# Diagonal convolution ahead, x1 and the first modal convolution between the taps: an interleaved state-space kernel on Trainium2

## The chip, the cores and the metric

The program runs on one core of one Trainium2 chip, in one launch, in fp32. The metric is device microseconds of that core. The engines are PE (TensorE matmul; PEld is its weight load), DVE (VectorE), ACT (ScalarE), POOL (GpSimd) and SP (SyncE, which issues nearly all transfers).

## The reference

```python
def _A_ref(q, k, v, shift_k, ssm_k, ssm_D):          # 2048 x 512
    ...                                              # k_shift: causal depthwise convolution of k, 4 taps
    kv = k_shift * v
    y = irfft(rfft(kv, 2 * S) * rfft(ssm_k, 2 * S))  # long causal convolution, channel by channel
    return q * (y + kv * ssm_D)

def _B_ref(u, log_A_real, A_imag, C_real, C_imag, log_dt, D_skip):
    A = -exp(log_A_real) + 1j * A_imag               # 512 channels x 128 modes
    C = (C_real + 1j * C_imag) * dt
    K = 2 * einsum("dn,dnl->dl", C, exp(A * dt * pos)).real      # the taps: 512 x 2048
    return irfft(rfft(u) * rfft(K)) + u * D_skip

x = A_q
x = x + _A_ref(_layernorm(x), ...)    # x1
x = x + _B_ref(_layernorm(x), ...)
x = x + _A_ref(_layernorm(x), ...)    # x2
x = x + _B_ref(_layernorm(x), ...)
```

The diagonal convolution y of kv is the same in both uses of A, and K is the same in both uses of B. So there is one diagonal convolution, one generation of K, two modal convolutions and two gated updates, x1 and x2.

## The kernel before

A convolution is a four-step FFT on PE with DVE's 32x32 transposes between steps, one quarter of the channels (128) at a time. The forward step (`fwd_group`, L173) multiplies by constant matrices and transposes into a spectrum tile z. Then come eight chunks: `f2_chunk` (L193) finishes the transform into PSUM (pu); ACT writes the swapped half into sw (L276, L277); DVE multiplies pu by the kernel's spectrum kab into vv (L278); POOL multiplies sw (L280), and POOL or DVE adds (L281); PE transforms back (pi, L290), ACT copies (L291). The way back out is four transposes into w (L305) and four pairs of matmuls (po, L311), each followed by the caller's `finish`. `convolution` (L250) writes this out as steps, with the chunks of neighbouring quarters overlapping.

Work before the convolutions:

- `taps` (L542) makes K in 64 taps of 8 channels by 4 and half the modes: exponentials (`mags`, L461, in batches of eight taps on ACT), rounded angles (`angles`, L474), sines (`waves`, L486), products on POOL and DVE (`products`, L497: L504, L505, L506, L508) and matmuls (`contract`, L511), whose result goes to DRAM.
- `spectrum_quarter` (L220) turns a quarter of a kernel into its spectrum, and DRAM holds it; for the modal kernel it can start when that quarter's 16 taps are in DRAM.
- `diagonal` (L658) is, in order: 48 steps of the four diagonal spectra, with the gates (`gated`, L600, which makes kv) and row statistics among them, and 59 steps of the diagonal convolution, whose output goes to DRAM (ya_d).

`run_steps` (L852) walks through two generators in turn, one step of `stream` (taps, and after each tap one step of a modal spectrum, if one is waiting) and two of `diagonal`. When both have ended come x1 (`gated_update`, L697: 16 row tiles, each gated with the loaded ya, then squares and statistics; `normalizer`, L203, twice), the first modal convolution (L831) and then, in new pools, x2 and the second modal convolution.

The written order is not the order of the engines. A planner simulates the program and orders each engine's instructions by priority (the written order) and by the time when operands and buffers are ready in its own clock; a tile is given out once all users of the buffer's earlier tile have ended. On the chip each engine and SP then go through their queues in that fixed order. `after` adds an order without a wait, which keeps exponentials and sines in batches on ACT.

Memory decides what can overlap: the pool `conv_a` of the diagonal part lies on the right side, and x takes its place; the pools of the taps lie on the left until `gctx.close()`. Of the eight PSUM banks, three are for convolutions ("c1"), two each for magnitudes and modal spectra ("pm") and for angles ("pa"), one for the taps' result.

Of the kernel before, what the change touches and what calls it, by code (L numbers as in the profile page):

```python
# [9 lines left out]
F32 = mybir.dt.float32  # L10
# [3 lines left out]
AF = mybir.ActivationFunctionType  # L14
# [85 lines left out]
def kernel(ctx: ExitStack, tc: tile.TileContext, out, x_in, kv_in, ssmk_in, ssmd_in,  # L100
# [5 lines left out]
    def sbuf(stack, name, side="left"):  # L106
        return stack.enter_context(tc.tile_pool(name=name, bufs=1, side=side, reuse_waits="tile"))
# [320 lines left out]
    psum["pm"] = (pp, NPM)  # L428

# [15 lines left out]
    NM1 = 9  # L445
    NM2 = 5
# [88 lines left out]
    zlast_k, todo = [], []  # L535
# [41 lines left out]

    def stream():
        for _ in taps():
            if todo and next(todo[0], 0) == 0:  # L580
                todo.pop(0)
            yield
        while todo:
            if next(todo[0], 0) == 0:
                todo.pop(0)
            yield


    with ExitStack() as actx:
# [100 lines left out]
    xp = sbuf(ctx, "xp", "right")  # L690
    x = xp.tile([128, 16, 512], F32, name="x")
    st = xp.tile([128, 16, 4, 6], F32, name="st")
    w1.append(xp.tile([128, 128], F32, name="w1"))
    nc.sync.dma_start(w1[0], w1_in)
    st_all = lambda t: st[:, t, :, :].rearrange("p q s -> p (q s)")

    def gated_update(buffer, spare, rnd, load_x=False):  # L697
        yas = []
# [41 lines left out]
    own = [(xp, "ut", 3)] * 3  # L740
# [5 lines left out]
    with ExitStack() as yctx:  # L746
        yp = sbuf(yctx, "yp", "right")
        normalized(gated_update(lambda k: yp.tile([128, 16, 4, 32], F32, name="yaq", tag="yaq", bufs=NYA),
                                own + [(yp, "ut", 16 - 4 * NYA)] * (16 - 4 * NYA), 0, True))
# [52 lines left out]
    def finish_b(rnd, q, g, po):  # L802
        xs = x[:, :, 128 * q + 32 * g:128 * q + 32 * g + 32]
        yo = xs
        if rnd == 1:
            pool, tag, bufs = own[0]
            yo = pool.tile([128, 16, 32], F32, name="yo", tag=tag, bufs=bufs)
# [23 lines left out]
    first = conv_b(0)  # L831
    for _ in range(2 * NCH):
        next(first)
    gctx.close()
    pctx.close()
# [10 lines left out]
    normalized(gated_update(lambda k: rotating("u", [128, 16, 4, 32], "yaq", 3),  # L846
                            own + [(pools["conv"], "vv", NSB)] * NSB + [(pools["conv"], "sw", NSB)] * NSB, 1))
    for _ in conv_b(1):
        pass


def run_steps(gens):  # L852
    gens = list(gens)
    while gens:
        for item in list(gens):
            for _ in range(item[1]):
                try:
                    next(item[0])
                except StopIteration:
                    gens.remove(item)  # L860
                    break
# [53 lines left out]
```

## Time and profile before

| what | us |
|---|---|
| median of 3 runs | 804.04 |
| lowest, highest | 797.04, 807.67 |
| the profiled execution | 805.59 |
| its span, first to last instruction | 803.8 |
| busy in the span: PE, DVE, POOL, ACT | 635.2, 621.3, 533.7, 477.7 |

Numbers of the profile come from that one execution. A row of grouped instructions gives line, engine, operation, output<-inputs, shapes, count, then busy time, mean length of one in ns, and the engine's idle time ahead of them with what ended it. Rows of one line give minimum, median and maximum in ns and the first and last start. Rows of stretches give from:to, length, then busy time and count for each engine, then the clock that was granted to PE, the DMA engines' share and GB/s; if only one line's instructions are asked for, one busy time stands there.

### The profile page before, as it was taken

What the parts mean: (1) busy time and instruction counts of PE and PEld (TensorE: products, weight loads), DVE (VectorE), ACT (ScalarE), POOL (GpSimd) and SP (SyncE); (2) the same over time, 40 slices, a digit from 0 to 9 for tenths busy, and PEclk for the clock granted to TensorE, in tenths of its full rate; (3) what the DMA queues carried; (4) which work ended last, traced back from release to release, by engine and by line L of the source; (5) the groups of instructions that cost most, each with busy time, mean ns of one, the idle gap of its engine ahead of it and who ended that gap; (6) DMA issues with size and microseconds to landing.
All of it is one profiled execution on the core that took longest, in us unless ns stands there. A gap on an engine that the chain in (4) does not pass through costs nothing. (4 is left out here: it accounts for less than half of the span.)

```text
span 803.8 us, 14448 instructions
## 1 busy us (share of the span) xinstructions
PE 635.2 (79%) x5064; PEld 447.3 (56%) x5064; DVE 621.3 (77%) x939; ACT 477.7 (59%) x879; POOL 533.7 (66%) x496
## 2 busy tenths in 40 slices
PE   3378696688799989999889863599789750998996
PEld 2255565356567747767556442386657620476673
DVE  7757979998967967647759499845668889878776
ACT  4035355345378875776785765649746525878573
POOL 4965778776778965838956277316665836288783
PEclk9676599868999999999899665789989995899999
DMA  9577177367477463664441593147987642068792
GB/s 326 188 247 270 40 241 254 108 200 254 146 215 203 127 182 110 182 171 123 115 131 34 174 341 105 46 129 199 233 200 183 159 103 54 1 164 223 201 252 105
DMA packets 89612, 135.47 MB, mean 169 GB/s; under 512 B 8508, under 2 KB 37700, under 8 KB 89028
## 3 DMA queue, kind: packets, MB, share of 16 engines
q1 hardware_dynamic: 88644, 132.13, 56.5%
q0 software_dynamic: 896, 2.43, 1.1%
q8 instruction: 40, 0.66, 0.4%
q14 instruction: 32, 0.26, 0.1%
HBM read 98.87 MB, written 35.65 MB: 167 GB/s over the span
## 5 line engine op out<-in xcount | busy, mean ns | idle before, releaser
L280 POOL TENSOR_TENSOR sw<-sw,kab 128x512 f32<-128x512 f32 x96 | 124.4, 1302 | 67.6 <-ACT sw L277 59.6
L196 PEld LDWEIGHTS pu<-zu,w 128*128 128x128 f32 x768 | 95.7, 193 | 52.9 <-DVE vv L278 18.6
L196 PE MATMUL pu<-zu,w 128*128 128x128 f32 x768 | 109.5, 285 | 15.1 <-DVE vv L278 12.8
L504 POOL TENSOR_TENSOR xy<-tt,m 128x512 f32<-128x512 f32 x64 | 84.9, 1327 | 53.5 <-ACT tt L493 23.8
L171 PE MATMUL pf<-kk,wz 128*128 128x256 f32 x256 | 86.3, 481 | 41.8 <-POOL kk L236 25.3
L278 DVE TENSOR_TENSOR vv<-pu,kab 128x512 f32<-128x512 f32 x96 | 64.9, 679 | 63.9 <-ACT sw L277 27.0
L290 PE MATMUL pi<-vv,mm 128*128 128x128 f32 x768 | 107.3, 285 | 3.5 <-DVE vv L278 2.6
L281 POOL TENSOR_TENSOR vv<-vv,sw 128x512 f32<-128x512 f32 x76 | 98.8, 1303 | 13.6 <-DVE vv L278 10.3
L290 PEld LDWEIGHTS pi<-vv,mm 128*128 128x128 f32 x768 | 96.5, 197 | 15.0 <-issue 9.1
L276 ACT ACTIVATE sw<-pu 64x512 f32<-64x512 f32 x96 | 57.0, 594 | 63.3 <-PE pu L196 60.8
L171 PEld LDWEIGHTS pf<-kk,wz 128*128 128x128 f32 x256 | 56.7, 237 | 62.3 <-POOL kk L236 33.3
L491 ACT ACTIVATE tt<-pa 128x512 f32<-128x512 f32 x64 | 38.3, 599 | 82.1 <-PE pa L483 72.3
L196 PE MATMUL pu<-zk,w 128*128 128x128 f32 x512 | 78.3, 307 | 6.4 <-DVE zk L191 4.2
L196 PEld LDWEIGHTS pu<-zk,w 128*128 128x128 f32 x512 | 72.7, 217 | 15.6 <-DVE zk L191 6.3
L505 DVE TENSOR_TENSOR tt<-tt,m 128x512 f32<-128x512 f32 x64 | 79.9, 1248 | 0.9 <-ACT tt L493 0.4
L244 ACT COPY pc<-pu 128x512 f32<-128x512 f32 x64 | 37.4, 591 | 57.3 <-PE pu L196 35.3
L506 DVE SCALAR_TENSOR_TENSOR xy<-tt,m 128x256 f32<-128x256 f32 x64 | 51.5, 805 | 25.7 <-ACT tt L492 15.3
L468 ACT ACTIVATE m<-pm 128x512 f32<-128x512 f32 x96 | 53.8, 604 | 22.6 <-PE pm L466 21.6
L483 PE MATMUL pa<-y,minus 128*128 128x512 f32 x64 | 37.1, 588 | 32.0 <-DVE y L482 30.5
L311 PE MATMUL po<-w,w 128*64 128x512 f32 x192 | 55.4, 655 | 7.3 <-DVE w L305 7.0
L519 PE MATMUL pk<-xy,tt 128*32 128x64 f32 x2048 | 50.5, 242 | 13.3 <-DVE ks L529 9.0
L519 PEld LDWEIGHTS pk<-xy,tt 128*32 128x32 f32 x2048 | 37.7, 122 | 39.1 <-issue 28.9
(139 smaller groups left out, 1295.4 us busy)
## 6 DMA issues: line engine op xcount, KB each, us to landing
kab<-spec SPq DMA_DIRECT2D x188, 256.0 KB, 4.0
spec<-pc SPq DMA_DIRECT2D x64, 256.0 KB, 2.7
kvt<-kv_in SPq DMA_DIRECT2D x16, 624.0 KB
yaq<-ya_d SPq DMA_DIRECT2D x8, 1024.0 KB, 10.6
kk<-ssmk_in SPq DMA_DIRECT2D x16, 256.0 KB, 2.9
kv_d<-u SPq DMA_DIRECT2D x16, 256.0 KB, 7.5
kdram<-ks SPq DMA_DIRECT2D x64, 64.0 KB, 1.8
kk<-kdram SPq DMA_DIRECT2D x16, 256.0 KB, 2.7
```

The lines of the kernel that those rows point to most:

```text
L171: yield T.matmul(o, w, rhs, start=True, stop=True)
L196: ins = T.matmul(pu[:, i, :], w2[:, c * CK + i, :], z[:, :, c * CK + i, :], start=True, stop=True)
L276: S.mul(sw[0:64], pu[64:128], -1.0)
L278: V.tensor_mul(vv, pu, kabs[s][:, 0])
L280: (V if last else G).tensor_mul(sw, sw, kabs[s][:, 1])
L281: (V if last or s % add_dve == add_dve - 1 else G).tensor_add(vv, vv, sw)
L290: i1s[t] = T.matmul(pi[:, i, :], mm[:, c * CK + i, :], vvs[t][:, i, :], start=True, stop=True)
L311: ins = T.matmul(po[64 * a:64 * a + 64], w4, ws[g][:, :, 16 * a:16 * a + 16, :].rearrange("p x t r -> p t x r"), start=True, stop=True, ti ...
L468: i = S.activation(m, pm, AF.Exp)
L504: G.tensor_mul(xy[:, :, :, 32:64], tt[:, :, :, 1:33], m1[:, :, 32:64][:, None].to_broadcast([128, 2, 8, 32]))
L505: (G if (4 * gi + k) % E2P == E2P - 1 else V).tensor_mul(e2, e2, m2[:, None].to_broadcast([128, 2, 8, 32]))
L519: T.matmul(pk[32 * i4:32 * i4 + 32, 2 * k + i, :], e2[:, r, 4 * i + i4, :], xy[:, r, 4 * i + i4, :], start=r == 0, stop=r == 1, tile_posit ...
```

## The change

`run_steps` goes. One generator, `main`, now holds the diagonal part, x1 and a newly written first modal convolution, `conv_b0`, and it takes three steps for each step of `stream` while the stream's step number is under 34, then two. x's pool is opened when the diagonal pool is closed, while the taps' pools stay open.

`conv_b0` works quarter by quarter with one z: the results of the way back replace z's chunks in place, and the next quarter's z is a new tile in the same buffer. Chunks have a lag of one, kab three buffers (the w tiles of the way out take theirs too), sw and vv two. A quarter begins its chunks when its modal spectrum has been written (`spectra`). It uses the full-height forward matrices throughout, where the earlier one used half-height ones from its second quarter on. Quarters 0 to 2 use the "c1" banks; the last one uses the taps' banks for pi and po. Row statistics of quarter q - 1 and the normalization of q + 1 go with the chunks of q. To make room, the magnitudes get 8 and 4 buffers in place of 9 and 5, and raw rows one in place of two.

```diff
-    NM1 = 9
-    NM2 = 5
+    NM1 = 8
+    NM2 = 4
...
-        raw = wk.tile([128, 2, 128], F32, name="raw", tag="raw", bufs=2)
+        raw = wk.tile([128, 2, 128], F32, name="raw", tag="raw", bufs=1)
...
-        RT = 1
-        RD = 2
-        diag = diagonal()
-        for _ in range(4):
-            next(diag)
-        run_steps([(stream(), RT), (diag, RD)])
...
+        yield from diagonal()
+        actx.close()
...
+    def conv_b0():
...
+        NK0 = 3
+        LAG0 = 1
...
+        def load(q, c):
+            kab = bp.tile([128, 2, CK, 128], F32, name="kab", tag="kab", bufs=NK0)
+            for h in range(2):
+                nc.sync.dma_start(kab[64 * h:64 * h + 64].rearrange("p r k c -> p r (k c)"),
+                                  spec[1][q][c].rearrange("(r k) x -> k r x", r=2))
...
+        def chunk(q, c):
+            kab = kabs[q, c]
+            pu, _ = f2_chunk(zs[q], c)
+            sw = bp.tile([128, CK, 128], F32, name="sw", tag="sw", bufs=2)
+            vv = bp.tile([128, CK, 128], F32, name="vv", tag="vv", bufs=2)
+            S.mul(sw[0:64], pu[64:128], -1.0)
+            S.copy(sw[64:128], pu[0:64])
+            V.tensor_mul(vv, pu, kab[:, 0])
+            G.tensor_mul(sw, sw, kab[:, 1])
+            (V if c % 3 == 2 else G).tensor_add(vv, vv, sw)
+            vvs[q, c] = vv
+
+        def back(q, c):
+            pi = bank("pi", "pa" if q == NQ - 1 else "c1").rearrange("p (k c) -> p k c", k=CK)
+            for i in range(CK):
+                T.matmul(pi[:, i, :], mm[:, c * CK + i, :], vvs[q, c][:, i, :], start=True, stop=True)
+            S.copy(zs[q][:, :, c * CK:(c + 1) * CK, :], pi.rearrange("p k (x r) -> p x k r", r=2))
...
+        for q in range(NQ):
+            zs[q] = bp.tile([128, 64, 32, 2], F32, name="zu", tag="z", bufs=1)
+            for g in range(4):
+                fwd_group(lambda ps_, j, n: us[q][ps_, :, 32 * g + j:32 * g + j + n], zs[q], 32 * g, 32, 16)
+                yield
+            while spectra[0] <= q:
+                yield
+            for c in range(-2, NCH + LAG0):
+                if c + 2 < NCH:
+                    load(q, c + 2)
+                if 0 <= c < NCH:
+                    chunk(q, c)
+                    if q < NQ - 1:
+                        norm(q + 1, c)
...
+                if c >= LAG0:
+                    back(q, c - LAG0)
+                if c >= 0:
+                    yield
+            for g in range(5):
+                if g < 4:
+                    turn(q, g)
+                if g > 0:
+                    out_group(q, g - 1)
+                yield
...
+    steps = main()
+    for _ in range(4):
+        next(steps)
+    RD = lambda n: 3 if n < 34 else 2
+    n = 0
+    for _ in stream():
+        for _ in range(RD(n)):
+            next(steps, None)
+        n += 1
+    for _ in steps:
+        pass
+    gctx.close()
+    pctx.close()
...
-    first = conv_b(0)
-    for _ in range(2 * NCH):
-        next(first)
-    gctx.close()
-    pctx.close()
...
-    for _ in first:
-        pass
```

`turn` and `out_group` are the transposes into w and the output matmuls, whose sum DVE adds to x.

More of the change, by code (lines that the diff above doesn't have):

```diff
@@ L428 @@
     psum["pm"] = (pp, NPM)
+    psum["pa"] = (pp, NPA)
     for tag, bufs in (("c1", 7 - NPA - NPM), ("pa", NPA), ("pk", 1)):
@@ L533, in contract @@
                 ks[32 * i4:32 * i4 + 32].rearrange("p (s t) c -> p s (t c)", s=4))
-    zlast_k, todo = [], []
+    zlast_k, todo, spectra = [], [], [0]
     EORD = 3
@@ L576, in taps, with spectrum_step, first_half @@
             yield
+    def spectrum_step():
+        if todo and next(todo[0], 0) == 0:
+            todo.pop(0)
+            spectra[0] += 1
     def stream():
         for _ in taps():
-            if todo and next(todo[0], 0) == 0:
-                todo.pop(0)
+            spectrum_step()
             yield
         while todo:
-            if next(todo[0], 0) == 0:
-                todo.pop(0)
+            spectrum_step()
             yield
-    with ExitStack() as actx:
+    def first_half():
+        actx = ExitStack()
         ap = sbuf(actx, "conv_a", "right")
@@ L739 @@
     HN = 8
-    own = [(xp, "ut", 3)] * 3
+    own = lambda: [(bq, "ut", 3)] * 3
     def normalized(rows):
@@ new lines, in main @@
+    def main():
+        yield from first_half()
+        open_x()
+        with ExitStack() as yctx:
+            yp = sbuf(yctx, "yp", "right")
+            yield from normalized(gated_update(lambda k: yp.tile([128, 16, 4, 32], F32, name="yaq", tag="yaq", bufs=NYA),
+                                               [(yp, "ut", 7)] * 7, 0, True))
+        yield from conv_b0()
+    steps = main()
[7 more added lines that the diff above has]
+        n += 1
@@ L805, in finish_b @@
         if rnd == 1:
-            pool, tag, bufs = own[0]
+            pool, tag, bufs = own()[0]
             yo = pool.tile([128, 16, 32], F32, name="yo", tag=tag, bufs=bufs)
@@ L845 @@
         normalizer(t0, HN, st_all)
-    normalized(gated_update(lambda k: rotating("u", [128, 16, 4, 32], "yaq", 3),
-                            own + [(pools["conv"], "vv", NSB)] * NSB + [(pools["conv"], "sw", NSB)] * NSB, 1))
+    for _ in normalized(gated_update(lambda k: rotating("u", [128, 16, 4, 32], "yaq", 3),
+                                     own() + [(pools["conv"], "vv", NSB)] * NSB + [(pools["conv"], "sw", NSB)] * NSB, 1)):
+        pass
     for _ in conv_b(1):
         pass
[L852 to L861, printed above, removed]
 def _seq(a):
```

59 lines of the change are left out of this document (48 added, 11 removed).

## The prediction

> **What bounds the kernel now.** I read the page's busy shares first, then cut the span where the work changes (gates and spectra, diagonal convolution, x1, first modal convolution, and after x2 the second) and asked for busy time by stage.
>
> ```profile
> span 803.8 us, 14448 instructions
> PE 635.2 (79%) x5064; PEld 447.3 (56%) x5064; DVE 621.3 (77%) x939; ACT 477.7 (59%) x879; POOL 533.7 (66%) x496
> ```
> ```profile
> 40.00:230.00 190.00, 151.01 (x1276) 106.37 (x1277) 168.48 (x222) 87.94 (x152) 135.32 (x129) 0.82 0.61 198
> 230.00:465.00 235.00, 216.27 (x2059) 152.61 (x2057) 161.07 (x220) 172.91 (x300) 159.34 (x149) 0.94 0.51 146
> 465.00:517.00 52.00, 26.22 (x305) 17.75 (x305) 51.45 (x74) 28.11 (x61) 38.34 (x30) 0.63 0.54 162
> 517.00:657.00 140.00, 117.93 (x733) 87.44 (x732) 94.30 (x174) 84.72 (x165) 78.61 (x74) 0.94 0.65 166
> 693.00:804.00 111.00, 99.14 (x647) 69.04 (x646) 80.42 (x111) 73.67 (x140) 75.52 (x69) 0.99 0.63 171
> ```
>
> The columns are window, length, then busy time of PE, PEld, DVE, ACT and POOL, and the granted clock. S1 (gates, first kernel's spectra, taps) has DVE at 168 of 190. S2 (diagonal convolution and taps) has PE at 216 of 235, 92%. S3 (x1 and the last taps) has DVE at 51.5 of 52 and PE at half. S4 (last modal spectrum, first modal convolution) has PE at 118 of 140, 84%. Last, the second modal convolution has PE at 99 of 111, 89%. What DVE's time is made of, its rows tell:
>
> ```profile
> L505 DVE TENSOR_TENSOR tt<-tt,m x64: 643/1163/4292, 72.4 to 508.5; 128x512 f32<-128x512 f32 x64
> L506 DVE SCALAR_TENSOR_TENSOR xy<-tt,m x64: 375/462/3491, 71.4 to 512.8; 128x256 f32<-128x256 f32 x64
> L504 POOL TENSOR_TENSOR xy<-tt,m x64: 1171/1200/1718, 72.1 to 506.4; 128x512 f32<-128x512 f32 x64
> L508 POOL TENSOR_TENSOR xy<-tt,m x64: 667/880/1222, 73.2 to 508.0; 128x256 f32<-128x256 f32 x64
> L608 DVE TENSOR_TENSOR u<-kvt x15: 643/1145/2369, 18.2 to 218.3; 128x512 f32<-128x512 f32 x15
> L721 DVE SCALAR_TENSOR_TENSOR x<-ut,rs,x x32: 694/741/1950, 475.9 to 689.0; 128x512 f32<-128x512 f32 x32
> ```
>
> The same DVE instruction takes 643 ns or 4292 (minimum, median, maximum): DVE operations that read two SBUF tiles stretch, POOL's hardly do. I read that as DVE waiting for POOL, so I add POOL's busy time to DVE's two-input operations at their minimum. S1 has 25 taps (rows below) and some 14 gates of four such operations: 135 + 25 x 1.02 + 14 x 4 x 0.643 = 197 us in 190. S3: 38 + 6 x 1.02 + 16 x 0.694 = 56 in 52. Both are full. S4: 78.6 + 10 additions on DVE at L608's 0.643 = 85 in 140, so 61%. [...]
>
> How the taps and modal spectra lie in the stages (DVE's rounding, one for each tap; ACT's spectrum copies, eight a quarter, 32 of the first 36 being the other kernel's):
>
> ```profile
> 40.00:230.00 190.00, 16.55 (x25) 0.82 0.61 198
> 230.00:465.00 235.00, 21.80 (x33) 0.94 0.51 146
> 465.00:517.00 52.00, 3.91 (x6) 0.63 0.54 162
> ```
> ```profile
> 40.00:230.00 190.00, 21.29 (x36) 0.82 0.61 198
> 230.00:465.00 235.00, 9.33 (x16) 0.94 0.51 146
> 465.00:517.00 52.00, 2.12 (x4) 0.63 0.54 162
> 517.00:657.00 140.00, 4.68 (x8) 0.94 0.65 166
> ```
>
> **The change, in terms of PE and of that pair.** No computation goes away. In written order the diagonal part now gets three steps a tap, not two: its 48 steps of spectra and gates are through at tap 15, its 59 of convolution at tap 34. Then x1 takes taps 34 to 42, and the first modal convolution's quarters start at about 44, 53, 62 and, after the last spectrum, behind the taps. So S1 gives up taps, S2 too, and S4 gets them. PE's prices come from S2, grouped by line:
>
> ```profile
> L290 PE MATMUL pi<-vv,mm 128*128 128x128 f32 x256 | 37.3, 290 | 0.3 <-POOL vv L281 0.2
> L196 PE MATMUL pu<-zu,w 128*128 128x128 f32 x255 | 36.1, 282 | 0.6 <-DVE zu L191 0.5
> L171 PE MATMUL pf<-u,wz 128*128 128x256 f32 x96 | 26.8, 405 | 0.3 <-DVE zu L191 0.3
> L466 PE MATMUL pm<-tg,rw 64*128 64x512 f32 x58 | 26.8, 528 | 3.1 <-ACT m L468 2.5 <-ACT pc L244 0.6
> L519 PE MATMUL pk<-xy,tt 128*32 128x64 f32 x1056 | 24.6, 228 | 3.6 <-POOL xy L508 2.8 <-DVE y L482 0.8
> L196 PE MATMUL pu<-zk,w 128*128 128x128 f32 x144 | 21.1, 294 | 0.2 <-ACT m L468 0.2
> L311 PE MATMUL po<-w,w 128*64 128x512 f32 x64 | 19.8, 700 | 2.3 <-DVE w L305 2.3
> L483 PE MATMUL pa<-y,minus 128*128 128x512 f32 x33 | 17.7, 537 | 4.5 <-DVE y L482 4.3 <-ACT tt L491 0.2
> L171 PE MATMUL pf<-kk,wz 128*128 128x256 f32 x64 | 17.1, 395 | 1.5 <-DVE zk L191 1.4
> L478 PE MATMUL pa<-tt,rw 64*128 64x512 f32 x33 | 15.4, 490 | 2.4 <-ACT tt L492 2.4
> ```
>
> A tap: (26.8 + 24.6 + 17.7 + 15.4) / 33 = 2.56. A spectrum quarter: 64 x 21.1/144 + 17.1/2 = 17.9. A convolution quarter: (37.3 + 36.1 + 19.8)/4 + 26.8/3 = 32.2. All rows add to 243, PE was busy 216, since modelled spans of neighbours overlap: times 0.89, so 2.28, 16.0 and 28.7.
>
> - S1 loses 10 taps. It is full on the pair, and a tap takes 1.171 + 0.667 + 0.643 + 0.375 = 2.86 of it: 29 us, so 161.
> - S2 goes from 33 taps to 19 and from 2 spectrum quarters to 1.2: 14 x 2.28 + 0.8 x 16.0 = 45 us of PE, at 92% 49 us, so 186.
> - S3: x1 still waits for the whole diagonal output (layer norm over all channels) and for its loads. It stays at 52 with 6 taps beside it, because the pair is full with those. x1 ends at 40 + 161 + 186 + 52 = 439, not 517: 78 us earlier.
> - S4 gets 64 - 15 - 19 - 6 = 24 taps (54.7 us of PE), 1.3 more spectrum quarters (20.8), and a dearer forward step: quarters 1 to 3 used the half-array form below, 13.9/3 = 4.6 a quarter, and now take the 128x256 form, 8.9 x 0.89 = 8.0: 10 us. So 117.9 + 86 = 203 us of PE in place of 118. Its mix is now S2's, taps beside a convolution, so I take S2's 92%: 221 us, ending at 660. At the last stage's 89% it ends at 667, at S4's own 84% at 681.
>
> ```profile
> L171 PE MATMUL pf<-u,w 64*128 64x512 f32 x48 | 13.9, 629 | 0.0
> ```
>
> What follows 657 (statistics, x2, second convolution, 147 us) stays. The sum is +3 us on the profiled execution's 805.6 (1.8 outside the span): 809. Of the runs shown, 804.04 is the median, 1.6 below that execution.
>
> Costs that I put at nothing, with what covers them:
>
> ```profile
> kab<-spec SPq DMA_DIRECT2D x188, 256.0 KB, 4.0
> yaq<-ya_d SPq DMA_DIRECT2D x8, 1024.0 KB, 10.6
> ```
> ```profile
> ACT pc L244 <- DMA spec<-pc: 20.5, 7, 7.2
> ```
> ```profile
> L210 ACT ACT_TABLE_LOAD x2 | 2.6, 1283 | 0.0
> ```
>
> Eight magnitude buffers instead of nine, four instead of five: the last exponential of each batch of eight taps now waits for the previous tap's products, with ACT's sines and the convolution's copies queued behind it. Fewer buffers can gain nothing; the upper end is 8 batches x (1.20 + 0.88) = 17 us; I take 0, since some ten exponentials go ahead of it and ACT is 74% busy in S2. One raw buffer: 0, a load has four taps' time. x1's two square roots now fall among sines: 0 to two table loads each, 4 x 1.283 = 5.1, hidden by the pair in S3. The 64 kab loads of the first modal convolution move on SP in among row loads, tap stores and spectrum stores; a load waits there for one of three kab buffers, which the transposes use too, and behind it stand the stores that ACT's copies wait for. Those waits are 20.5 us now; from minus a few (two stores fewer at S4's start) to another 20.5; I take 0, as the diagonal convolution runs beside the taps with three such buffers. In front of x2 the new pool lies on the finished convolution's memory: 0 to one late load, 10.6; 0, for x2's second load is first used by its fifth row. Two additions move from DVE to POOL and two output groups the other way: under 3 us on engines with room.
>
> **The rivals.** *Faster: x1 gets filled.* If S3 took 14 taps, not 6 (PE's idle 25.8 us there would hold the 8 x 2.28 = 18), S4 loses 18/0.92 = 20 us: 789. If S4 then also reaches 95%, 203 - 18 = 185 takes 195 and not 201: 783. For it: before's S3 took every tap that was left, and 30 are now in stock. Against it: the pair, at 56 of 52. [...] Chance 0.27.
>
> *Slower: one z buffer makes the quarters a chain.* Each quarter's forward step now waits for the last transpose of the quarter before it, and two sw/vv buffers allow two chunks in flight.
>
> ```profile
> L276 ACT ACTIVATE sw<-pu 64x512 f32<-64x512 f32 x96 | 57.0, 594 | 63.3 <-PE pu L196 60.8 <-POOL vv L281 0.6 <-POOL sw L280 0.4
> L280 POOL TENSOR_TENSOR sw<-sw,kab x32: 1258/1282/1469, 232.2 to 423.1; 128x512 f32<-128x512 f32 x32
> L281 POOL TENSOR_TENSOR vv<-vv,sw 128x512 f32<-128x512 f32 x76 | 98.8, 1303 | 13.6 <-DVE vv L278 10.3
> L305 DVE STREAM_TRANSPOSE w<-ie 128x1024 f32<-128x1024 f32 x32 | 38.2, 1222 | 3.1 <-ACT ie L291 3.1
> L813 DVE TENSOR_TENSOR x<-x,po 128x512 f32<-128x512 f32 x14 | 9.5, 677 | 3.8 <-PE po L311 3.7
> ```
>
> A chunk is 8 matmuls each way (2 x 1.1), two ACT halves and a copy (3 x 0.59), two POOL operations (1.28 + 1.30): 6.6 us, so one each 3.0 with two in flight. A quarter alone: 8 x 3.0 + 3.6 + 8.0 forward + 4 x 1.22 + 1.9 to leave = 42. Beside taps S2's chunks came each 190.9/31 = 6.2 us, which makes 67. Two quarters beside taps and two behind them: 218, ending at 657, beside PE's 660. Once a third quarter runs at the tap pace, 25 us more: 685, +28, so 834; S4's own 84% gives 681, 830. It decides when the second quarter's last output comes later than the last tap. For it: both ends touch already, and S2 had two z buffers where this has one. Against it: PE would idle, and the taps would then be through sooner. Chance 0.29.
>
> *It doesn't do what it says.* The planner orders each engine by its own clock, and taps ran ahead of the written order before (58 begun by 465, against 52). If they do so wholly, the quarters come behind all taps: 4 x 42 = 168 in place of 140, plus 10 for the forward form: 843. Only the taps' own buffers hold them, but three wave tiles bind early. Chance 0.03.
>
> **How the numbers follow.** 809 is the likeliest, at 0.41, with its own range 797 to 820 (densities of 95% to 89% give 802 to 816, the small terms 4 or 5 more either way). Below it stands the filled x1, 783 to 789; above it the chain, 830 to 834, and the last, 843. About 0.1 is left out at each end by 780 to 838. What this measurement can tell from no change is 2%, so 788 to 820. Faster 0.27, within 0.41, slower 0.29 + 0.03 = 0.32.
>
> **What would show it.** In the changed profile, x1 should end near 439; taps after x1's end 24 in number; PE in the stretch from x1's end to the first convolution's end busy some 203 us at 92%; DVE's two-input products again between 0.64 and several us. POOL and two-input DVE time well under the stage's length in x1 while more than ten taps run there would make the first rival true. Chunks of the third quarter at 6 us and PE under 85% would show the chain. A last chunk of the first quarter behind the last tap would show the third. I am wrong at the root if S1 and S2 don't shorten by about 29 and 49 us, since all that S4 pays for comes from there.

## The result, and the profile after

The changed kernel takes 880.55 us (median of four runs, 871.81 to 886.3) against 802.79 for the kernel before beside it (797.04 to 807.67): a ratio of 1.0935, with a 95% interval of 1.0808 to 1.1062. One of the four executions of the changed kernel, 886.3, was in a slower state, and the ratio and its interval leave it out. The forecast was 809 us, 838 at the upper end. Below, times within the kernel and the bounds of stages belong to the profiled execution of after, 883.1 us with a span of 881.2.

The page's busy shares of after:

```profile
span 881.2 us, 14583 instructions
PE 667.0 (76%) x5112; PEld 477.5 (54%) x5112; DVE 624.9 (71%) x939; ACT 479.5 (54%) x879; POOL 535.1 (61%) x492
```

PE has 32 us more to do, DVE and POOL have nearly what they had; the span is 77 us longer. The stretches of after, cut where the same work begins and ends (window, length, then PE, PEld, DVE, ACT, POOL, clock, DMA share, GB/s):

```profile
40.00:230.00 190.00, 147.12 (x1275) 103.96 (x1274) 169.71 (x220) 85.45 (x149) 137.25 (x128) 0.81 0.61 199
230.00:465.00 235.00, 218.15 (x2040) 154.06 (x2039) 165.15 (x219) 168.62 (x291) 162.49 (x148) 0.93 0.50 140
465.00:519.00 54.00, 34.34 (x292) 22.12 (x293) 48.91 (x76) 36.33 (x71) 41.54 (x33) 0.56 0.65 192
519.00:735.00 216.00, 144.50 (x815) 114.33 (x813) 97.13 (x187) 84.69 (x164) 72.58 (x66) 0.84 0.36 93
768.00:881.00 113.00, 100.08 (x647) 69.72 (x645) 81.05 (x113) 73.71 (x140) 75.48 (x69) 0.98 0.61 168
```

S1 and S2 are what they were, within 4 us of PE's busy time. x1 ends at 519, where it ended at 518. The first modal convolution, S4, takes 216 us in place of 140 and PE is busy in 67% of it: 76 of the 77 us lie here. The taps of after, by stage (DVE's rounding, one a tap):

```profile
40.00:230.00 190.00, 16.49 (x25) 0.81 0.61 199
230.00:465.00 235.00, 21.69 (x33) 0.93 0.50 140
465.00:519.00 54.00, 3.90 (x6) 0.56 0.65 192
```

25, 33 and 6, exactly as before, and none beside the convolution. The text of the program now puts 15 taps beside the gates and spectra and 24 behind x1; the engines' order does not. So nothing was interleaved, and the newly written convolution had to run alone. What its engines wait for there (total us, times, longest):

```profile
DVE vv L792 <- ACT sw L791: 76.0, 28, 7.8
POOL sw L793 <- ACT sw L791: 68.6, 18, 18.1
PEld pi L800 <- POOL vv L794: 42.6, 17, 8.7
...
ACT zu L801 <- PE pi L800: 32.4, 22, 3.7
ACT u L770 <- PE pf L171: 31.1, 3, 15.5
```

Every engine waits for the one before it in a chunk's chain: ACT's swapped halves, POOL's product and addition, PE's way back, ACT's copy. The first quarter's end in the timeline (start, length, engine, line) shows the change to the second:

```profile
576.94 1.77 PE L800 MATMUL pi<-vv,mm 128*128 128x128 f32 x8 [2.42 <-POOL vv L794]
578.75 0.59 ACT L801 COPY zu<-pi 128x512 f32<-128x512 f32 x1 [3.60 <-PE pi L800]
579.37 3.50 DVE L805 STREAM_TRANSPOSE w<-zu 128x1024 f32<-128x1024 f32 x3 [4.44 <-ACT zu L801]
...
580.76 5.32 PE L811 MATMUL po<-w,w 128*64 128x512 f32 x16 [2.05 <-DVE w L805]
...
586.01 3.72 PE L171 MATMUL pf<-u,wz 128*128 128x256 f32 x16
...
590.92 3.84 PE L171 MATMUL pf<-u,wz 128*128 128x256 f32 x16 [1.19 <-DVE zu L191]
...
594.80 6.26 ACT L770 ACTIVATE u<-x,nb,rs 128x128 f32<-128x128 f32 x16 [15.46 <-PE pf L171]
...
601.07 0.59 ACT L790 ACTIVATE sw<-pu 64x512 f32<-64x512 f32 x1
```

After the last chunk come way back, copy, four transposes, output, the next forward step, and then all 16 normalizations of the quarter after that, on ACT, before its first swapped half: 28 us from the last swapped product of one quarter (574) to the first of the next (602). Before took 1 to 4 (the last and first products of neighbouring quarters on POOL).

### The profile page after: what moved, and what is told of

Same layout as the page of the kernel before. It is cut to its first block, busy times and chain, and to the rows that moved or that the text cites. A ratio compares the mean times of both kernels' runs of the same rounds, so it can differ in the third digit from the quotient of the medians.

```text
span 881.2 us, 14583 instructions
## 1 busy us (share of the span) xinstructions
PE 667.0 (76%) x5112; PEld 477.5 (54%) x5112; DVE 624.9 (71%) x939; ACT 479.5 (54%) x879; POOL 535.1 (61%) x492
## 5 line engine op out<-in xcount | busy, mean ns | idle before, releaser
L505 POOL TENSOR_TENSOR xy<-tt,m 128x512 f32<-128x512 f32 x64 | 87.6, 1369 | 49.3 <-ACT tt L494 35.9
L196 PEld LDWEIGHTS pu<-zu,w 128*128 128x128 f32 x768 | 99.6, 200 | 32.3 <-issue 9.6
L171 PE MATMUL pf<-kk,wz 128*128 128x256 f32 x256 | 83.6, 471 | 40.2 <-POOL kk L236 26.7
L506 DVE TENSOR_TENSOR tt<-tt,m 128x512 f32<-128x512 f32 x64 | 82.2, 1285 | 0.9 <-ACT tt L494 0.8
L171 PE MATMUL pf<-u,wz 128*128 128x256 f32 x264 | 71.1, 412 | 11.7 <-DVE zu L191 5.4
L800 PE MATMUL pi<-vv,mm 128*128 128x128 f32 x256 | 43.6, 326 | 46.3 <-POOL vv L794 39.3
L281 POOL TENSOR_TENSOR vv<-vv,sw 128x512 f32<-128x512 f32 x54 | 70.6, 1310 | 10.5 <-DVE vv L278 8.7
L290 PE MATMUL pi<-vv,mm 128*128 128x128 f32 x512 | 72.9, 288 | 0.7 <-POOL vv L281 0.3
L290 PEld LDWEIGHTS pi<-vv,mm 128*128 128x128 f32 x512 | 65.2, 199 | 9.0 <-issue 4.5
L507 DVE SCALAR_TENSOR_TENSOR xy<-tt,m 128x256 f32<-128x256 f32 x64 | 56.9, 890 | 16.6 <-ACT tt L493 15.0
L800 PEld LDWEIGHTS pi<-vv,mm 128*128 128x128 f32 x256 | 38.3, 230 | 50.7 <-POOL vv L794 42.6
```

The costliest lines, as they stand in the source:

```text
L171: yield T.matmul(o, w, rhs, start=True, stop=True)
L196: ins = T.matmul(pu[:, i, :], w2[:, c * CK + i, :], z[:, :, c * CK + i, :], start=True, stop=True)
L281: (V if last or s % add_dve == add_dve - 1 else G).tensor_add(vv, vv, sw)
L290: i1s[t] = T.matmul(pi[:, i, :], mm[:, c * CK + i, :], vvs[t][:, i, :], start=True, stop=True)
L505: G.tensor_mul(xy[:, :, :, 32:64], tt[:, :, :, 1:33], m1[:, :, 32:64][:, None].to_broadcast([128, 2, 8, 32]))
L506: (G if (4 * gi + k) % E2P == E2P - 1 else V).tensor_mul(e2, e2, m2[:, None].to_broadcast([128, 2, 8, 32]))
```

## Experiments

The place of the quarters tells most. Below, from the traces: the end of x1, the start on POOL of each quarter's first swapped product, and the end of the last addition to x.

| kernel | end of x1 | first products of the four quarters | end | median us |
|---|---|---|---|---|
| before | 518 | 545, 571, 598, 626 | 657 | 802.8 |
| after | 519 | 549, 602, 654, 701 | 733 | 880.6 |
| e1_rd2 | 519 | 550, 603, 655, 702 | 734 | 879.2 |
| e8_rd9 | 492 | 526, 589, 641, 687 | 720 | 872.8 |
| e2_oldconv | 512 | 545, 571, 598, 627 | 658 | 806.6 |
| e3_z2 | 514 | 564, 617, 668, 715 | 746 | 897.5 |
| e5_z2early | 518 | 569, 614, 659, 703 | 735 | 882.5 |
| e7_normedge | 512 | 535, 580, 625, 672 | 705 | 858.2 |
| e9_spread | 516 | 562, 606, 650, 694 | 726 | 874.7 |
| e10_banks | 511 | 556, 596, 641, 684 | 720 | 873.8 |
| e11_lag | 519 | 565, 604, 642, 680 | 708 | 854.4 |
| e12_both | 509 | 554, 587, 621, 656 | 685 | 838.1 |
| e14_cross | 519 | 564, 591, 619, 646 | 676 | 825.3 |
| e4_hold34 | 459 | 498, 579, 653, 701 | 733 | 882.6 |
| e13_hold_edge | 459 | 495, 567, 647, 696 | 728 | 875.9 |

In after, e2_oldconv, e3_z2, e5_z2early, e7_normedge, e9_spread to e12_both and e14_cross, PE, DVE, ACT and POOL run the same instructions in the same order through the first 440 us, and yet x1 ends anywhere from 509 to 519: that is the scatter of single executions. So a first product is best read from the end of x1, and a quarter from the one before it.

**Does the written ratio move the taps?** Two steps a tap throughout, in the changed kernel:

```diff
-    RD = lambda n: 3 if n < 34 else 2
+    RD = lambda n: 2
```

> The changed kernel with two steps of main for each tap throughout, instead of three for the first 34. Theory P (the planner places taps by readiness in its own clock, the written ratio hardly moves them, and the first modal convolution therefore stands behind all taps): within 1% of the changed kernel, 872 to 889 us, last tap again near 505, first chunk of the first modal convolution again near 549. Rival W (the ratio of three is what the changed kernel pays for): 10 us or more away from the changed kernel, and the taps lie elsewhere.

879.22 us, 1.0993 [1.0936, 1.1049]; 26, 32 and 6 taps in the three stages. Then the other way, the diagonal part written almost wholly ahead of the taps:

```diff
-    RD = lambda n: 3 if n < 34 else 2
+    RD = lambda n: 9 if n < 11 else 0 if n < 33 else 4 if n == 33 else 2
```

> The changed kernel with the diagonal part written wholly ahead of tap 12 (nine steps a tap, then none up to tap 33; x1 from tap 34 as before). Theory P (the planner places by readiness, a written ratio does not hold taps back): the taps lie as in the changed kernel, over 55 of them done when the diagonal convolution ends, 870 to 892 us. Rival W2 (a stronger ratio does displace taps): under 50 taps done by then, the diagonal convolution ends before 440, and the time moves by 10 us or more.

872.8 us, 1.0841 [1.078, 1.0902]. The taps of e8_rd9 by stage:

```profile
40.00:230.00 190.00, 15.85 (x24) 0.84 0.59 193
230.00:465.00 235.00, 22.67 (x34) 0.94 0.55 152
465.00:519.00 54.00, 2.40 (x4) 0.61 0.55 165
519.00:735.00 216.00, 1.63 (x3) 0.85 0.43 106
```

24 and 34, then six (one rounding lies across 519 and is counted on both sides). From two steps a tap to nine, 58 taps have been begun by 465, and the last swapped product of the diagonal convolution's chunks starts behind 52 of them in e1_rd2 and behind 50 in e8_rd9, whose text puts it ahead of tap 12 (only the last four steps of the diagonal part come later, at tap 34). The ratio is a priority, and for these taps the priority hardly decides. In the traces the last transpose of the diagonal convolution's output stands behind the roundings of 56 taps in e1_rd2 and of 53 in e8_rd9; in the ten kernels named above the order of PE, DVE, ACT and POOL stayed the same while the times scattered, so I take it that this was settled when the program was built. The last six taps, however, did move: in e8_rd9 they begin at 505 to 529, behind x1, which ends at 492 and not at 519. So the first quarter does lie beside taps there, its eight chunks take 31 us instead of 25 from the first swapped product to the last, and 8 of those 27 us are left in the median. Why the planner's clock finds a tap ready before a chunk so often, no run here shows.

**Is it the frame or the new convolution?** The change's generator, steps, pools and smaller buffers, but the earlier first modal convolution behind the taps:

```diff
-        yield from conv_b0()
...
+    first = conv_b(0)
+    for _ in range(2 * NCH):
+        next(first)
     gctx.close()
     pctx.close()
...
+    for _ in first:
+        pass
```

> The changed kernel with its frame kept (one generator, three steps then two, x's pool opened early, 8 and 4 magnitude buffers, one raw buffer), but the first modal convolution is the earlier one again, with its own spectra tiles, lag of four and five sw/vv buffers. Theory P (all of the loss is the new convolution's own length, 214 us from the end of x1 to its last output against 140): 797 to 815 us. Rival B (fewer buffers for the taps, the earlier pool, or the ratio cost a part): above 825 us.

806.59 us, 1.0078 [1.0043, 1.0112]. Its S4:

```profile
519.00:659.00 140.00, 116.88 (x728) 86.78 (x728) 91.96 (x167) 79.61 (x150) 79.32 (x76) 0.93 0.68 168
```

140 us as before for a stretch cut at the same times. In this execution x1 ends at 512 already; from the first swapped product to the end are 112.5 us, 112.1 in before. The frame costs 0.8%, at most 1.1%; the rest is `conv_b0`.

**What makes `conv_b0` slow?** First a second z buffer. For the room, the taps' pools are closed ahead of the convolution in this kernel, in e5_z2early, in e9_spread and in all that are built on e9_spread; no tap runs beside it (above), so no overlap with taps is given up. But the last modal spectrum is, since the closing moves the convolution behind the loop over `stream`: in these seven kernels the forward step of quarter 0 begins on PE 33 us behind x1's end, in after 8 and in before 10, and the first swapped product comes 45 to 51 us behind x1's end, in after 30 and in before 28. In e3_z2 DVE's first normalization waits 14.8 us for ACT's last copy of a spectrum.

```diff
-            zs[q] = bp.tile([128, 64, 32, 2], F32, name="zu", tag="z", bufs=1)
+            zs[q] = bp.tile([128, 64, 32, 2], F32, name="zu", tag="z", bufs=2)
...
-        yield from conv_b0()
...
     gctx.close()
+    for _ in conv_b0():
+        pass
     pctx.close()
```

> The changed kernel with two z buffers for the new convolution; to make room, the taps' SBUF pools are closed ahead of it, which in the changed kernel it comes behind anyway. Theory Z (one z buffer: from the last chunk of a quarter to the first of the next pass 28 us, 574 to 602, where the earlier convolution took under 7): three changes of quarter save some 20 us each, 805 to 835 us. Rival L (lag of one and two sw/vv buffers make the chain): above 860 us, the gaps between quarters stay.

897.53 us, 1.124 [1.1185, 1.1294], slower still. The quarters stay 52 us apart, and the convolution starts 15 us later (564 for 549), 20 if read from x1's end, by the closing. The buffer alone unties nothing, since the forward step is still written behind the way out. With that written ahead of the way out too:

```diff
+            if q < NQ - 1:
+                yield from forward(q + 1)
             for g in range(5):
                 if g < 4:
                     turn(q, g)
```

> Two z buffers as in the run before (which moved nothing: 897.5 us, quarters still 52 us apart), and the next quarter's forward step is written ahead of this quarter's transposes and outputs. Theory O (what ties the quarters is the written order through the three banks they take in turn: the forward step's banks come behind the output groups' banks; z is a second tie): the forward step goes beside the drain of the last chunk, the change of quarter falls from 28 us to some 19, total 860 to 878 us. Rival N (the tie is something else, such as normalization or the loads): stays within 10 us of 897.

882.54 us, 1.0967 [1.0924, 1.101]: 15 us better than e3_z2, the quarters 45 apart. Apart from this, in the changed kernel itself, the 16 normalizations at the change of quarter were put behind the swapped copies of the chunks beside which they are written:

```diff
+        copied = [None]
...
-                    S.activation(o, i, AF.Identity, scale=rs[:, t:t + 1], bias=nb[:, t:t + 1])
+                    n = S.activation(o, i, AF.Identity, scale=rs[:, t:t + 1], bias=nb[:, t:t + 1])
+                    if q > 0:
+                        after(n, copied[0])
...
-            S.copy(sw[64:128], pu[0:64])
+            copied[0] = S.copy(sw[64:128], pu[0:64])
```

> The changed kernel with one edge of order on ACT: the normalizations of the next quarter, 16 in a row for 6.3 us ahead of a quarter's first chunk (594.8 to 601.1), go behind the swapped copy of the chunk they are written with. One z, order of steps unchanged. Theory O prices that row at 3 x 6.3 us: 855 to 870 us. Rival N2 (they fill a wait that something else causes): 876 us or more.

858.22 us, 1.0671 [1.0624, 1.0718]. With one u buffer the next quarter's normalizations had stood ahead of the first swapped half of quarters 0, 1 and 2 (three waits of `ACT u` in the table of waits). Without them the second and third quarter start 45 us after the one before, not 52, and the first starts at 535, not 549; the fourth, which normalizes for nobody, keeps its 47. Of the 14 us at the start, 7 lie ahead of x1's end (512 for 519, the scatter of one execution); behind it the first product comes after 23 us, not 30, and that is about the 6.26 of ACT. From x1's end to the end of the convolution the gain is 20 us. Both together (two z buffers and this order), with the next forward step spread among the last chunks and the normalizations among the first four:

```diff
+                if c >= 5 and q < NQ - 1:
+                    group(q + 1, c - 5)
...
-                    if q < NQ - 1:
-                        norm(q + 1, c)
+                    if q < NQ - 1 and c < 4:
+                        norm(q + 1, 2 * c)
+                        norm(q + 1, 2 * c + 1)
```

> Two z buffers, the next quarter's forward groups written between this quarter's last chunks, its normalizations among the first four chunks and behind their copies; lag of one and two sw/vv buffers kept. Theory O: the change of quarter all but goes, a quarter takes 27 to 32 us in place of 52, total 897 less 3 x 22 = 820 to 842 us. Rival L (lag and two buffers make the chain): above 860 us.

874.68 us, 1.0848 [1.0791, 1.0904]. The change of quarter shrank from 28 us to some 15 (591 to 606), but the eight chunks stretched from 25 to 29, and the quarters are still 44 apart. Three chunks of the second quarter in e9_spread's timeline:

```profile
614.33 1.35 PE L804 MATMUL pi<-vv,mm 128*128 128x128 f32 x8
...
615.52 1.06 PE L196 MATMUL pu<-zu,w 128*128 128x128 f32 x8
...
618.10 1.13 PE L804 MATMUL pi<-vv,mm 128*128 128x128 f32 x8 [1.53 <-ACT zu L805]
...
619.07 1.06 PE L196 MATMUL pu<-zu,w 128*128 128x128 f32 x8
...
621.98 1.16 PE L804 MATMUL pi<-vv,mm 128*128 128x128 f32 x8 [1.85 <-POOL vv L798]
...
622.97 1.06 PE L196 MATMUL pu<-zu,w 128*128 128x128 f32 x8
```

PE goes strictly back and forth, one way back, one chunk, and stands still between: 3.8 us a chunk for 2.2 us of matmuls. Either the three PSUM banks (one pool for pu, pi, pf and po) or the lag of one chunk with two sw and vv buffers could force that. Three kernels on e9_spread separate them. Eight banks:

```diff
+    pctx.close()
+    with tc.tile_pool(name="ps1", bufs=1, space=PSUM, reuse_waits="tile") as pp1:
+        psum["c1"] = (pp1, 8)
+        for _ in conv_b0():
+            pass
```

> The kernel with two z buffers, spread normalizations and early forward steps (e9_spread, 874.7 us, quarters 44 us apart), and only this changed: the first modal convolution gets eight PSUM banks for pu, pi, pf and po in place of three. Theory B (with three banks, the transform of a chunk waits for the bank of an earlier one, so two chunks are in flight whatever else is there): the quarters go to some 30 us, near the 28 that before takes (112 us from the first swapped product to the end, four quarters), so 820 to 835. Theory L (the lag of one chunk and two sw and vv buffers bind): still some 44 us apart, 865 to 880. Theory M (both bind, each alone hides the other): 855 to 878.

A lag of three, five sw, vv and kab buffers:

```diff
-        NK0 = 3
-        LAG0 = 1
+        NK0 = 5
+        LAG0 = 3
...
-            sw = bp.tile([128, CK, 128], F32, name="sw", tag="sw", bufs=2)
-            vv = bp.tile([128, CK, 128], F32, name="vv", tag="vv", bufs=2)
+            sw = bp.tile([128, CK, 128], F32, name="sw", tag="sw", bufs=5)
+            vv = bp.tile([128, CK, 128], F32, name="vv", tag="vv", bufs=5)
```

> e9_spread with three banks kept, but a lag of three chunks between a chunk and its way back, five sw and five vv buffers in place of two, and five kab buffers in place of three. Theory L: quarters of some 30 us, 820 to 835. Theory B: no gain, 865 to 885. Theory M: 855 to 878.

And both edits in one kernel:

> e9_spread with both: eight banks, a lag of three, five sw, vv and kab buffers. All three theories expect quarters of some 30 us here: first swapped product at 562 as in e9_spread, and 112 us to the end as in before, so the convolution ends near 675 and the whole at 820 to 835. Should the quarters stay over 40 us apart, all three fall, and what remains is ACT's own order: normalizations, swapped halves and copies in one queue.

Banks alone 873.8 us, 1.0892 [1.0817, 1.0966], nothing; lag and buffers alone 854.39, 1.0648 [1.057, 1.0727]; both 838.12, 1.0462 [1.039, 1.0534]. The lag with its buffers (sw, vv and kab, not separated) binds first, at some 20 us, a little beyond what I had allowed for a case in which both bind; behind it the banks are worth another 16 by the medians, 12 by the time from the first product to the end (143 and 131 us). With both, the quarters are 33 to 35 apart, just above the 820 to 835 expected. At their change, in e12_both:

```profile
576.79 0.59 ACT L805 COPY zu<-pi 128x512 f32<-128x512 f32 x1 [2.03 <-PE pi L804]
...
579.60 5.36 PE L825 MATMUL po<-w,w 128*64 128x512 f32 x16 [1.96 <-DVE w L809]
...
584.89 3.84 PE L196 MATMUL pu<-zu,w 128*128 128x128 f32 x32
```

The next quarter's spectrum has been ready since 576.6 (the last `zu<-pf` transpose, 575.9 for 0.72), but its first chunk stands on PE behind the way out of the quarter before, which waits for ACT's copy and DVE's transposes: 15 us from the last swapped product to the next (572.7 to 587.5). So the way out was written among the next quarter's chunks, with two w buffers of its own (order and buffers were not separated):

```diff
+                if q > 0 and 0 <= c < 5:
+                    way_out(q - 1, c)
                 if c >= LAG0:
                     back(q, c - LAG0)
...
-            for g in range(5):
+            for g in range(5) if q == NQ - 1 else ():
```

> The kernel with eight banks, a lag of three and five buffers (e12_both, 838.1 us, quarters 33 to 34 us apart where before takes 28), changed only in the written order: the way out of a quarter (its four transposes into w and its output matmuls) is written among the first five chunks of the next quarter, as before writes it, not ahead of them; its row statistics follow at chunks 5 to 7, and w gets two buffers of its own. In the trace of e12_both the first chunk's matmuls of the second quarter start at 584.9, right behind the last output matmul, though their spectrum was ready at 576.6. Theory W (PE's fixed order, with the way out ahead of the chunks, is what remains): a change of quarter shrinks from 14 us to about 7, three times, so 812 to 824. Theory S (what remains is the pace of the chunks and the later start, 554 against 545): no gain at the changes that lasts, 832 to 842.

825.33 us, 1.0311 [1.0257, 1.0366], 13 us less and a hair above the range of Theory W. The change of quarter takes 6 to 7 us, and the convolution from its first swapped product on, in e14_cross:

```profile
564.00:675.00 111.00, 99.14 (x654) 78.47 (x653) 80.65 (x143) 74.67 (x143) 74.79 (x65) 0.98 0.60 155
```

111 us, where before takes 112 (545 to 657). The new convolution is now as fast as the old one, and what is left of the loss, a span of 824.2 against 803.8, is its start: 564 against 545. On PE of e14_cross the forward step of quarter 0 (`pf<-u`) comes behind all of the last modal spectrum (`pu<-zk`):

```profile
545.91 2.08 PE L196 MATMUL pu<-zk,w 128*128 128x128 f32 x8 [2.16 <-ACT pc L244]
551.78 9.10 PE L171 MATMUL pf<-u,wz 128*128 128x256 f32 x32 [3.80 <-ACT u L772]
```

In before the two alternate:

```profile
527.14 3.20 PE L171 MATMUL pf<-u,wz 128*128 128x256 f32 x12
530.17 1.95 PE L196 MATMUL pu<-zk,w 128*128 128x128 f32 x16
```

All seven kernels that close the taps' pools ahead of the convolution start like this, 45 to 51 us behind x1's end, and the others outside the two with held taps 23 to 34 us: so, as far as these runs show, this rest comes with the closing, by which the experiments made room for their buffers, and not from the loop of `conv_b0`. Whether these 19 us can be had back with the buffers kept was not tried.

**And if the taps are really held back?** In the changed kernel, the taps from number 34 on were ordered on PE behind the last output matmul of the diagonal convolution (`diag_last`):

```diff
-        T.matmul(pa, rows[gi][hs, 0, :], ...)
+        first = T.matmul(pa, rows[gi][hs, 0, :], ...)
+        if 4 * gi + k >= 34:
+            after(first, diag_last[0])
```

> The changed kernel with the interleaving forced: taps 34 to 63 are ordered on PE behind the last output matmul of the diagonal convolution, so that they do lie beside x1 and the first modal convolution. Theory S (the sum of the prediction: the diagonal convolution is held up by the taps' PE work, so its stage shortens by some 49 us when 20 taps leave it): the diagonal convolution ends near 415, x1 near 470, total 800 to 835 us. Rival C (the diagonal convolution goes at the pace of its own chain and buffers, whatever lies beside it): it ends near 450 as before, the held taps come on top, total 870 to 930 us.

882.6 us, 1.1039 [1.1001, 1.1078]: the same time as after, in quite another shape. Stretches of e4_hold34 (the rest of S2, x1, the two quarters beside taps, the two behind them):

```profile
230.00:415.00 185.00, 155.89 (x1155) 112.44 (x1154) 96.79 (x127) 105.89 (x182) 109.33 (x99) 0.90 0.52 145
415.00:460.00 45.00, 22.97 (x222) 12.41 (x221) 42.97 (x71) 33.15 (x67) 34.43 (x26) 0.50 0.75 223
460.00:633.00 173.00, 141.07 (x1361) 102.78 (x1360) 119.20 (x183) 112.59 (x208) 92.75 (x89) 0.87 0.34 91
633.00:735.00 102.00, 70.79 (x402) 55.72 (x400) 48.80 (x97) 37.79 (x70) 36.25 (x34) 0.85 0.41 107
```

and its taps in the same stretches, 22 of them behind x1:

```profile
230.00:415.00 185.00, 7.24 (x11) 0.90 0.52 145
415.00:460.00 45.00, 4.08 (x6) 0.50 0.75 223
460.00:735.00 275.00, 14.30 (x22) 0.86 0.37 97
```

x1 ends at 459, 60 us earlier, and all of it is lost again before the convolution's end at 733: PE has 211.87 us of work between 460 and 735, 77% of the time. Beside the taps PE is busy in 82% of the time (141.07 of 173), in the two quarters behind them in 69%. Last, this hold together with e7_normedge's order of normalizations:

> Two edits together: the taps from 34 on held behind the diagonal convolution (e4_hold34, 882.6 us) and each normalization of the next quarter ordered behind the swapped copy of its chunk (e7_normedge, 858.2, against 880.55 without). The question is what paces the quarters while taps lie between them. Theory C (the quarters' own chain of forward step, normalizations and chunks paces them, taps or none): the edge is worth here what it was there, some 22 us, so 856 to 868. Theory T (where taps are left, engine queues shared with them pace the quarters, and the edge helps only the two quarters behind the taps): half of it, 869 to 877. Theory N (the taps' work fills what the edge frees): nothing, 878 to 887.

875.93 us, 1.0862 [1.0788, 1.0937]: in Theory T's range. That is 7 us by the medians, some 14 by the two ratios (1.1039 and 1.0862): a third to two thirds of the 22 that the order was worth without taps. The second quarter starts 9 us earlier (72 behind the first, not 81), of which the first quarter's chunks make 6 (35 to 29 us); but the change from the second quarter to the third gives 7 back (36 to 43), with the second quarter's chunks as long as before (38 and 37). So with taps between them the quarters are not paced by that part of their chain alone; which of the shared queues paces them stays open.

## Why the prediction was wrong

**The step that failed is the first: that the written order moves the taps.** "S1 gives up taps, S2 too, and S4 gets them" did not happen; S1 and S2 shortened by nothing, not by 29 and 49, which the prediction itself named as its root. What it gave a chance of 0.03, that the planner orders by its own clock and the quarters come behind all taps, is what happened; that no ratio from two to nine steps draws the bulk of the taps out of S1 and S2 is shown by e1_rd2 and e8_rd9. I had the evidence in hand (58 taps begun by 465, against 52 in the written order) and took it for a small deviation, on the ground that the taps' own buffers would hold them. By these ratios, the written order in before was simply near the one that the planner would have chosen; a trace of one order does not show how far it depends on the text. Nor would the taps alone have saved the forecast: with them held back, e4_hold34 takes 882.6 us, so the density of 92% for S4 is a second step that failed (below).

**That rival's price was too low, 843 for 880.** It was 4 x 42 + 10 = 178 for a stage that takes 214 from x1's end to the last addition. Its terms hold two slips that nearly cancel: half of a chunk's 6.6 us is 3.3, not 3.0, which makes a quarter 45 (after shows 3.3 to 3.6 from one product to the next, 23 to 25 us over seven); and the 42 has the dearer forward step's 8.0 in it already, so that the 10 counts it twice. What is missing is elsewhere. The 30 us from x1's end to the first swapped product (519 to 549, 28 in before) were counted only as far as the forward step's 8: 22 us. The rest lies at the changes of quarter. The quarters come 47 to 53 us apart; the 28 us at a change hold 6.26 of normalizations that I had not placed there, with the next quarter's u in a single buffer behind the forward step. The dearer forward step was rightly seen (11 us: 33.0 of PE's time for 13.9 and 7.8 in before). That PE's busy time there is 144.5 us for 117.9 before has a second reason: the way back's matmuls are longer there, 326 ns for 288, 7.5 us in all (below).

**The slower rival had the mechanism, not the key.** One z buffer making a chain of the quarters, with two chunks in flight, describes the trace well. But z's single buffer is only one link: e3_z2 takes it away and gains nothing. The links that count are the lag with its few buffers (20 us, e11_lag), the banks behind it (12 to 16, e12_both) and the order of way out, forward step and normalizations (e5_z2early, e7_normedge, e14_cross: 13 to 22 each). I had put no price on three PSUM banks for four kinds of tile.

**The amounts of work hold, once the taps are really held; the densities don't.** In e4_hold34 S2 has 22 taps less and one spectrum quarter less, by its rows of ACT's spectrum copies:

```profile
230.00:415.00 185.00, 4.60 (x8) 0.90 0.52 145
415.00:460.00 45.00, 0.00 (x0) 0.50 0.75 223
460.00:735.00 275.00, 11.49 (x20) 0.86 0.37 97
```

By the prediction's prices that is 22 x 2.28 + 16.0 = 66 us of PE; measured are 216.27 - 155.89 = 60. But PE is busy in 84% of what is left, not 92%, so that S2 ends 50 us earlier and not 66 / 0.92 = 72. x1 with 6 taps takes 45 (52 predicted). Behind x1, 22 taps and 1.5 spectrum quarters more than before make 117.9 + 50 + 24 + 10 = 202 by the prices, and 212 measured. There the density, 92% taken over from S2 because the mix was the same, is 77%: at that, the prediction's own 203 us would have made S4 264 long, 43 us more than the 221 that it took. Two things are in this figure. Beside taps, where the mix is S2's, PE is busy in 82%; in the two quarters behind the taps, for which the prediction used 92% as well, in 69%, much as in after without any taps (67%). In S2 the convolution had two z buffers and a lag of two; in `conv_b0` it has one of each. That this makes the difference beside taps is argued from the runs without taps; no run here has held taps and the deeper buffers together.

**What was put at nothing** (smaller magnitude and raw buffers, table loads, kab loads, the late load) is in e2_oldconv: 1.0078, some 6 us, within the bounds of 0 to 17 that the buffers alone had. **The faster rival** wasn't tested by the change, as x1 had the same six taps. In e4_hold34, with 28 taps in stock at 415, x1 again took six, with DVE at 43 of 45 us. That fits the pair, POOL's busy time and DVE's two-input operations, as the prediction held against it. That DVE waits for POOL, the trace of before shows: 43 of the 64 `tt<-tt,m` take 0.84 us or more, and each of these ends 0.29 to 0.55 us behind the end of a POOL operation (at 249.85 one takes 1.69, beside POOL's 1.39 from 249.60), while the 96 `vv<-pu,kab`, which read PSUM, all take 0.64 to 0.69, 87 of them beside a POOL operation. That the two times simply add up was an estimate, and no run shows it: in x1 of e4_hold34 the sum is 34.4 + 6 x 1.02 + 16 x 0.694 = 52 us in 45. And the planner sets which taps lie there, so it is not shown that the pair kept more out. The interleaving took place in e4_hold34 and e13_hold_edge, and of the 60 us gained ahead of the convolution all were given back in the first, and all but 5 in the second (875.9 for 880.6).

## What to carry to other kernels

Where a planner orders the engines, a change of the written order is a request: ask of the planned order of one engine, or of a run with the ratio turned to its extremes, whether anything moves before pricing what would follow. A stage's density belongs to its buffers, banks and lag as much as to its mix of work (PE's 92% in S2 of before, 82% beside taps in e4_hold34); when work is moved into a smaller copy of a stage, price the copy by its own chain of one item, times the number that its tightest resource lets fly. And when memory forces a lean version of a loop, first run the lean version alone: here it cost 76 us by itself, more than the 60 by which x1 came earlier once the taps were held back.

## What was not expected of the hardware

The same 128x128 matmul of the way back took 326 ns in after and 288 in before. Before and after, in the stage of the first modal convolution (busy time, mean ns of one, then PE's idle time just ahead):

```profile
L290 PE MATMUL pi<-vv,mm 128*128 128x128 f32 x256 | 36.1, 288 | 3.2 <-DVE vv L278 2.6 <-POOL vv L281 0.4 <-ACT ie L291 0.2
L196 PE MATMUL pu<-zu,w 128*128 128x128 f32 x256 | 37.4, 289 | 10.4 <-DVE vv L278 10.2
```
```profile
L800 PE MATMUL pi<-vv,mm 128*128 128x128 f32 x256 | 43.6, 326 | 46.3 <-POOL vv L794 39.3 <-DVE vv L794 7.0
L196 PE MATMUL pu<-zu,w 128*128 128x128 f32 x256 | 36.0, 287 | 2.9 <-DVE zu L191 2.4 <-DVE vv L792 0.3
```

288 and 326 ns, with 3.2 and 46.3 us of idle time ahead of them and a mean granted clock of 0.94 and 0.84 in the stage. The chunks' other 128x128 matmul, `pu<-zu`, mostly follows without a gap in after (2.9 us of idle time), and it did not get longer: 289 and 287 ns. What goes with their length in the traces is the clock granted at their start: 72 of the 256 `pi<-vv` of after started at 0.5 and took 427 ns in the mean, 184 at 1.0 and took 286; in before 16 at 0.5 took 430, 240 at 1.0 took 279. Of after's `pu<-zu` only 24 started at 0.5 (404 ns; the other 232 took 275). So here the mean clock of a stage does not lengthen all of its matmuls alike; the way back is busy for 7.5 us more in all. In e14_cross, whose convolution has PE busy in 89% of its time, the clock stands at 0.98. The three pairs of busy share and clock (67% and 0.84, 84% and 0.94, 89% and 0.98) agree in direction, though S2 of before, 92% busy at 0.94, lies off their line, and no run here was made to separate cause from effect.
